# Moving one set of weight sums forward on GpSimd, and one column copy's engine, in a chunked attention with a Fourier mix and an MLP

## The chip, the cores and the metric

The kernel runs on one core of a Trainium2 chip. The metric is the device time of one launch in microseconds (us); the median of three runs is compared. All arithmetic is in fp32.

## The reference

What is computed, cut to what matters:

```python
# attention inside chunks of 64 tokens; q, k, v are (8, 8, 576, 64)
scores = (q_c @ k_c^T) / sqrt(64)
attn = softmax(scores)                    # over the chunk's 64 keys
x = (attn @ v_c) -> (8, 576, 512)         # heads side by side
# Fourier mix
mixed = real(fft(fft(x, axis=1), axis=2))
u = x + mixed
# normalisation over 512, then an MLP 512 -> 2048 -> 512, and the sum
un = (u - mean(u)) / sqrt(var(u) + 1e-6)
out = u + relu(un @ w_ch1) @ w_ch2
```

The two weights arrive as float64 and are converted to fp32 on the chip.

## The kernel before

**Tiles and groups.** Tokens are handled in tiles of 128 rows. A batch has four tiles, two of kind "lo" and two of kind "hi"; every even batch is preceded by one tile of kind "rest", which holds the middle chunks of two batches. The list `tiles` has them in order, and `first[b]` is the index of the first tile of batch b: `first[1]` is 5, `first[2]` is 9, and tile 9 is ("rest", 2, 0). Group g of the MLP is the four tiles of batch g (the last group: the four rest tiles).

**Stages.** While TensorE works at the MLP of group g, the attention and the Fourier mix of the next batch are woven in between its steps. The counter `t` numbers the steps of all groups; `begin[g]` is the first step of group g, and `begin[1]` is 32. The order of instructions on each engine is the order in which the Python code issues them, since the schedule is written out by hand; every engine works through its own queue in that order. SP issues most of the transfers, ScalarE a few.

**Attention.** `att_T` turns q and k of the next tile: from tile 10 on VectorE transposes them (L416), and for a "lo" tile a column copy on GpSimd follows (L418). For tile 9 and below TensorE transposes them (L397) and ScalarE copies the result, with the column copy on ScalarE or GpSimd (L428 to L431). `att_S` makes the scores (`sc`, L448), `softmax` and `exponential` follow, `att_P` turns the result, `att_V` makes the output (`xp`, L498), which VectorE scales and writes to `xall` (L511 to L515). `load` fetches q and k of the tile after (L250 in its second form), each into a buffer that has only one copy, so that a load of q waits for the transpose of the q before it.

**The MLP with saved products.** Group 0 goes through the plain product (`up_first`, `down_plain`). The down product of group 0 fills four PSUM banks `dn`, and at its end VectorE adds the residual and evicts them (L1249); `store` then writes the tiles out, "lo" tiles with L1037, "hi" tiles with L1046, on SP's queue and in part on ScalarE's.

From group 1 on, both products use a scheme with seven half-size products in place of eight. It needs sums of blocks of both weights, which GpSimd makes once:

- `keep2(i)`, i = 0 to 3: four sums over blocks of the second weight (L1087), written to `xall` (odd i) or `yall` (even i) and from there stored to a table in DRAM by SP (L1091). It is a generator that yields after each sum.
- `keep1(pair)`, pair = 0 to 3: four sums over blocks of the first weight (L1069), two written over parts of the second weight's space in `wb` that is free by then, one in place in `wa`, one more in `wb`. Group 1 uses them from there, and `keep1_store` saves them for later groups (L1074).
- `combined`: the like sums of the activations, on VectorE (L1024 to L1026, and L1022 for the late part of group 1).

`up_halves(1)` begins with product 1, whose weight is the second sum of `keep1(0)`: its first products are `pb` (L1289), then `pa`. The banks `pa` and `pb` come from the same ring of four as the `dn` banks.

**Where the sums are issued.** Once all pieces of the weights are converted, each step advances `conv2` by three: this chain runs `keep2` in the order 1, 0, 3, 2. What is left of it is issued at the end of step `begin[1] - 1`, and after it `keep1(0)`; the other three sets of `keep1` follow at steps 33, 35 and 37:

```python
conv2 = iter([step for i in range(HF // 2) for step in [keep2(i ^ 1)]])
...
if t == begin[1] - 1:
    for _ in conv2:
        pass
if begin[1] - 1 <= t < begin[1] + 7 and t % 2:
    keep1((t - begin[1] + 1) // 2)
```

So GpSimd's queue has, in this order: `keep2(1)`, `keep2(0)`, `keep2(3)`, `keep2(2)` with a column copy (L418) in `keep2(3)`, a memset (L528) in `keep2(2)` and another column copy (L418) behind it, then `keep1(0)`, `keep1(1)`, `keep1(2)`, the row shifts of `shift` (L555), and `keep1(3)`.

Of the kernel before, what the change touches and what calls it, by code (L numbers as in the profile page):

```python
# [16 lines left out]
def kernel(  # L17
# [85 lines left out]
    NO, HF = 7, KF // 2  # L103
# [63 lines left out]
    tiles, first = [], []  # L167
# [27 lines left out]
    def kind(n):  # L195
        return tiles[n][0]
# [196 lines left out]
    def turn(src):  # L393

        pt = ps_t.tile([128, 4, 128], FP32, tag="pt", name="pt")
        for j in range(4):
            nc.tensor.transpose(pt[:, j, :], src(j), ident)  # L397
        return pt


    def att_T(n, which="qk"):

        if n > first[2]:
            for src, dst, nm in ((qs, qT, "qT"), (ks, kT, "kT")):
                if nm[0] not in which:
                    continue
                a = src.pop(n).rearrange("p j (t b d) -> p j t b d", t=4, b=2)[:, :, :, 0]  # L410
                t = one_p.tile([128, NJ, 2, CH + 1], FP32, tag=nm, name=nm)
                low = kind(n) == LO and nm == "qT"
                to = t[:, :, :, CH:0:-1] if low else t[:, :, :, 0:CH]
                if kind(n) == HI:
                    to = to[:, :, ::-1]
                nc.vector.transpose(out=to.rearrange("p j c (r t) -> p j t c r", t=4), in_=a)  # L416
                if low:
                    nc.gpsimd.tensor_copy(t[:, :, :, 0:1], t[:, :, :, CH:CH + 1])  # L418
                dst[n] = t.rearrange("p j c t -> p (j c) t")
            if n + 1 < NT:  # L420
                load(n + 1, which)
            return
        a = qs.pop(n)
        pt = turn(lambda j: a[:, 2 * j:2 * j + 2, :].rearrange("p h d -> p (h d)"))
        t = one_p.tile([128, 2 * NJ, CH + 1], FP32, tag="qT", name="qT")
        low = kind(n) == LO
        nc.scalar.copy(t[:, :, CH:0:-1] if low else t[:, :, 0:CH], pt.rearrange("p j (c t) -> p (j c) t", c=2))
        if low and n < first[1]:  # L428
            nc.scalar.copy(t[:, :, 0:1], t[:, :, CH:CH + 1])
        elif low:  # L430
            nc.gpsimd.tensor_copy(t[:, :, 0:1], t[:, :, CH:CH + 1])  # L431
        qT[n] = t
        a2 = ks.pop(n)
        pt = turn(lambda j: a2[:, 2 * j:2 * j + 2, :].rearrange("p h d -> p (h d)"))
        t = one_p.tile([128, NJ, 128], FP32, tag="kT", name="kT")
        nc.scalar.copy(t, pt)
        kT[n] = t.rearrange("p j (c t) -> p (j c) t", c=2)
        if first[1] <= n + 1 < NT:
            load(n + 1)
# [617 lines left out]
    def parts1(pair):  # L1057
        a11, a12, a21, a22 = w1_part(pair, 0, 0), w1_part(pair, 0, 2), w1_part(pair, 1, 0), w1_part(pair, 1, 2)
        o1, o2, o4 = (made1(pair, j) for j in range(3))
        return a11, o2, o1, a21, a12, o4, a22  # L1060

    def keep1(pair):

        a11, o2, o1, a21, a12, o4, a22 = parts1(pair)
        for out_, in0, in1, op in (
            (o1, a21, a22, ALU.add), (o2, o1, a11, ALU.subtract),
            (a21, a11, a21, ALU.subtract), (o4, a12, o2, ALU.subtract),
        ):
            nc.gpsimd.tensor_tensor(out=out_, in0=in0, in1=in1, op=op)  # L1069
# [6 lines left out]
    def keep2(i):  # L1076

        m = 2 * i
        b11, b12 = w2[:, m:m + 2, 0:HM], w2[:, m:m + 2, HM:DM]
        b21, b22 = w2[:, HF + m:HF + m + 2, 0:HM], w2[:, HF + m:HF + m + 2, HM:DM]  # L1080
        to = xall[:, 2 * G:2 * G + 4, 0:DM] if i % 2 else yall
        o1, o2, o3, o4 = (to[:, j].rearrange("p (m e) -> p m e", m=2) for j in range(4))
        for out_, in0, in1, op in (
            (o1, b12, b11, ALU.subtract), (o2, b22, o1, ALU.subtract),
            (o3, b22, b12, ALU.subtract), (o4, b21, o2, ALU.subtract),
        ):
            nc.gpsimd.tensor_tensor(out=out_, in0=in0, in1=in1, op=op)  # L1087
            yield
        to = s2.rearrange("o p (m e) -> o p m e", m=HF)
        for o, a in ((1, o2), (2, o1), (3, o3), (6, o4)):  # L1090
            nc.sync.dma_start(out=to[o, :, m:m + 2], in_=a)  # L1091
        yield

    def keep2_whole(i):

        m = 2 * i
        to = s2.rearrange("o p (m e) -> o p m e", m=HF)
        for o, m0, e0 in ((0, m, 0), (4, HF + m, 0), (5, HF + m, HM)):
            nc.sync.dma_start(out=to[o, :, m:m + 2], in_=w2[:, m0:m0 + 2, e0:e0 + HM])
# [331 lines left out]
    def mlp(g):  # L1431

        for h1 in up_halves(g) if g >= first_of[1] else up_plain(g) if g > 0 else up_first():
            yield
        yield from (down_few if g >= FEW else down_halves if g >= first_of[2] else down_plain)(g, h1)

    with tc.manual_schedule():
# [33 lines left out]
        def round_next(later=None):  # L1471
            nonlocal n_w
            if n_w <= len(pieces):
                round_weight(n_w, later)
                n_w += 1
# [22 lines left out]
        begin = [0]  # L1498
        for g in range(NG):
            begin.append(begin[-1] + (KF if g < first_of[1] else 2 * HF) + (KF if g < first_of[2] else 2 * NO if g < FEW else NR2 // 2))  # L1500
        ready_at = [begin[g] + (2 * KF - 7 if g < first_of[2] else 2 * HF + 4) for g in range(NG)]
        conv2 = iter([step for i in range(HF // 2) for step in [keep2(i ^ 1)]])

        def chain(gens):
            for gen in gens:
                yield from gen

        n_whole, n_kept, late, rest_ = 0, 0, [], None
        conv2 = chain(conv2)
        t = 0  # L1510
        for g in range(NG):
            for _ in mlp(g):
                t += 1
                heavy = False
                for do in late:
                    do()
                late = []
                if t == 8:
                    nc.scalar.copy(tk, early_tk[:, :, :, 0:NE])
                if cur < len(sides):  # L1520
                    t0 = 3 if cur == 0 else ready_at[cur - 1]
                    t1 = ready_at[cur]
                    due = min(sizes[cur], (t - t0) * sizes[cur] // (t1 - t0))
                    while done < due:
                        heavy = next(sides[cur], None) or heavy
                        done += 1
                    if t >= t1:
                        for _ in sides[cur]:
                            pass
                        cur, done = cur + 1, 0  # L1530
                if not heavy:
                    round_next(late if t < KF and t % 4 == 3 else None)
                    if t <= 2 or t < KF and t % 4 == 0 or t >= KF + 3:
                        round_next()

                while n_whole < HF // 2 and n_w > KF + HF + 2 * n_whole + 2:
                    keep2_whole(n_whole)
                    n_whole += 1
                if n_w > len(pieces):
                    for _ in range(3):  # L1540
                        next(conv2, None)
                if t == begin[1] - 1:
                    for _ in conv2:
                        pass
                if begin[1] - 1 <= t < begin[1] + 7 and t % 2:
                    keep1((t - begin[1] + 1) // 2)
                if t == ready_at[NG - 3]:
                    rest_ = make_rest()
                    next(rest_)
                if t > ready_at[NG - 3] + 4 and (t < begin[NG - 2] or t % 4 != 3):  # L1550
                    next(rest_, None)
                if t == begin[FEW] + 2:
                    more = [xall[:, 2 * G:2 * G + 4, :].rearrange("p a f -> p (a f)")[:, i * Z3:(i + 1) * Z3] for i in range(2)]
                    more += [one_p.tile([128, Z3], FP32, tag=tag, name="more") for tag in ("q", "k", "zf")]
                    slab3.extend(a.rearrange("p (m e) -> p m e", m=4) for a in more)
                if begin[FEW] + 2 <= t < begin[FEW] + 2 + NS3:
                    fetch(3)
                if begin[1] < t < begin[1] + KF:
                    for i in range(2):
                        if n_kept < HF // 2 * NO:  # L1560
                            keep1_store(n_kept)
                            n_kept += 1
                if t in (begin[1] + 9, begin[1] + 13, begin[1] + 16):
                    fetch(2)
                if t == begin[1] + KF:
                    for _ in range(NS1):
                        fetch(1)
# [49 lines left out]
```

## Time and profile before

| | |
|---|---|
| median of three runs | 1073.49 us (1072.22 to 1073.67) |
| the profiled execution, its own time | 1074.23 us |
| its span | 1072.2 us |
| TensorE busy | 1046.3 us, 98% of the span |
| VectorE busy | 610.8 us, 57% |
| GpSimd busy | 406.6 us, 38% |
| ScalarE busy | 315.3 us, 29% |
| end of group 0's down product on TensorE | 190.37 us |
| first product of group 1 on TensorE | 192.78 us |

The span reaches from the first instruction to the last; some 2 us of the time lie around it. The profile is one execution, so single rows are right for that execution, and the median of the runs may lie a little to either side. PE is TensorE, DVE VectorE, ACT ScalarE, POOL GpSimd; SPq and ACTq are the engines' issue queues. A time "at 190.37" is counted from the span's start. A share of busy time is an average over stages with different limits: what a change in one stage is worth is read from the waits of that stage.

### The profile page before, as it was taken

The numbers are of one execution on the slowest core, as the hardware profiler recorded it, in microseconds if no ns is written. First come the engines' busy times: TensorE is split into PE (matmuls) and PEld (weight loads), VectorE is DVE, ScalarE is ACT, GpSimd is POOL, SyncE is SP. The second block draws the span as 40 slices with busy tenths as digits, with TensorE's granted clock in tenths as the row PEclk, the third lists the DMA queues.
The fourth block names the chain that finished last, engine by engine and source line by source line (L and its number), as shares of the span: only waits on it lengthen the run. The fifth ranks groups of instructions, "written<-read, shape, count | busy, mean of one in ns | idle before, by whom it ended". The sixth has DMA issues, their size and how long they took to land.

```text
span 1072.2 us, 20212 instructions
## 1 busy us (share of the span) xinstructions
PE 1046.3 (98%) x7498; PEld 854.6 (80%) x7498; DVE 610.8 (57%) x1319; ACT 315.3 (29%) x746; POOL 406.6 (38%) x531
## 2 busy tenths in 40 slices
PE   8999989899999999999999999999999999999997
PEld 6645444688888888888888888788888888888886
DVE  4798986684567465664565554745664535433331
ACT  4688563233113411322032312331133103101200
POOL 4310018672415140344134321614161726780281
PEclk9999999999999999999999999999999999999999
DMA  8767565489668546883667266954654559776763
GB/s 176 232 186 218 123 196 189 139 249 312 233 199 232 149 140 198 239 232 119 191 209 231 99 182 195 231 165 163 202 177 116 208 191 350 229 231 199 272 228 106
DMA packets 157759, 212.74 MB, mean 198 GB/s; under 512 B 69308, under 2 KB 103100, under 8 KB 151390
## 3 DMA queue, kind: packets, MB, share of 16 engines
q1 hardware_dynamic: 154012, 208.04, 63.4%
q10 hardware_dynamic: 3330, 2.76, 1.1%
q8 instruction: 60, 0.98, 0.4%
q0 software_dynamic: 320, 0.66, 0.3%
q14 instruction: 37, 0.30, 0.1%
HBM read 177.31 MB, written 34.08 MB: 197 GB/s over the span
## 4 chain that ended last, share of the span: by engine, by line
PE 77%; DVE 8%; DMA 5%; ACT 4%; SPq 3%; issue 2%; POOL 1%; DVEq 0%; ACTq 0%; POOLq 0%
PE pa L1289 19%; PE pb L1341 18%; PE pb L1289 14%; PE pa L1341 13%; PE dn L1405 4%; PE pt L397 2%; PE mix L838 2%; DMA xall<-in_moe_w_ch_dram 1%; SPq L263 1%; PE xp L498 1%; PE z L719 1%; DVE power L378 1%; DMA out_dram<-o 1%; PE sc L448 1%; DMA v<-in_v_dram 1%
## 5 line engine op out<-in xcount | busy, mean ns | idle before, releaser
L1289 PE MATMUL pa<-unT,wa 128*128 128x256 f32 x736 | 175.0, 381 | 2.5 <-DVE wa L1297 2.5
L1289 PEld LDWEIGHTS pa<-unT,wa 128*128 128x128 f32 x736 | 138.3, 190 | 21.8 <-DVE wa L1297 2.7
L1289 PE MATMUL pb<-wa 128*128 128x256 f32 x448 | 106.9, 381 | 0.1
L1341 PE MATMUL pa<-wb,h 128*128 128x256 f32 x448 | 101.5, 380 | 0.0
L1341 PE MATMUL pb<-wb,h 128*128 128x256 f32 x448 | 100.7, 379 | 0.0
L1289 PEld LDWEIGHTS pb<-wa 128*128 128x128 f32 x448 | 84.1, 190 | 12.3 <-DVE h L1299 0.5
L1341 PEld LDWEIGHTS pa<-wb,h 128*128 128x128 f32 x448 | 83.9, 190 | 11.3
L1341 PEld LDWEIGHTS pb<-wb,h 128*128 128x128 f32 x448 | 84.1, 190 | 11.0
L1169 POOL TENSOR_TENSOR h<-h 128x256 f32<-128x256 f32 x56 | 47.7, 860 | 102.3 <-DVE wb L1167 98.2
L555 POOL COPY xall<-xall 1x512 f32<-1x512 f32 x28 | 17.8, 636 | 154.3 <-DVE xall L515 126.9
L1295 DVE TENSOR_TENSOR wa<-pb,wa 128x256 f32<-128x256 f32 x56 | 23.8, 425 | 69.7 <-ACT wa L1294 69.7
L1289 PE MATMUL pb<-unT,wa 128*128 128x256 f32 x256 | 60.5, 379 | 0.0
L1303 ACT ACTIVATE h<-pa 128x256 f32<-128x256 f32 x64 | 24.6, 384 | 114.1 <-PE pa L1289 113.6
L1236 PE MATMUL dn<-wb,h 128*128 128x512 f32 x128 | 57.5, 597 | 0.0
L1294 ACT COPY wa<-pa 128x256 f32<-128x256 f32 x56 | 20.9, 372 | 123.5 <-PE pa L1289 80.6
L1289 PEld LDWEIGHTS pb<-unT,wa 128*128 128x128 f32 x256 | 48.6, 190 | 6.6
L1289 PE MATMUL pa<-wa 128*128 128x256 f32 x224 | 53.9, 383 | 0.0
L1309 ACT ACTIVATE h<-h 128x512 f32<-128x512 f32 x64 | 39.6, 629 | 45.0 <-DVE h L1308 44.8
L1341 PE MATMUL pb<-wb,yall 128*128 128x256 f32 x224 | 51.2, 381 | 0.0
L1341 PE MATMUL pa<-wb,yall 128*128 128x256 f32 x224 | 50.6, 379 | 0.3 <-DMA wb<-s 0.3
L1341 PE MATMUL pb<-wb 128*128 128x256 f32 x224 | 50.7, 379 | 0.0
L1195 PE MATMUL up<-unT,wa 128*128 128x512 f32 x108 | 49.4, 598 | 0.0
(299 smaller groups left out, 1976.1 us busy)
## 6 DMA issues: line engine op xcount, KB each, us to landing
wb<-s SPq DMA_DIRECT2D x49, 1024.0 KB
wa<-s SPq DMA_DIRECT2D x196, 256.0 KB
xall<-in_moe_w_ch_dram SPq DMA_DIRECT2D x22, 512.0 KB
q<-in_q_dram SPq DMA_DIRECT2D x96, 112.0 KB
k<-in_k_dram SPq DMA_DIRECT2D x96, 112.0 KB
wb<-s SPq DMA_DIRECT2D x16, 512.0 KB
v<-in_v_dram SPq DMA_DIRECT2D x124, 64.0 KB
s<-part SPq DMA_DIRECT2D x30, 256.0 KB
```

What stands on the lines that cost most here:

```text
L397: nc.tensor.transpose(pt[:, j, :], src(j), ident)
L838: nc.tensor.matmul(out=mix[:, cols], lhsT=zt[:, T], rhs=tab, start=(T == 0), stop=(T == 3), skip_group_check=True,)
L1169: nc.gpsimd.tensor_tensor(out=h1[:, m, hi], in0=h1[:, m, lo], in1=h1[:, m, hi], op=ALU.subtract)
L1195: nc.tensor.matmul(out=up, lhsT=w1[:, kk, m * 128:(m + 1) * 128], rhs=unT[:, kk], start=(kk == 0), stop=(kk == KD - 1), skip_group_check=True,
L1236: nc.tensor.matmul(out=dn, lhsT=h1[:, m, s * 128:(s + 1) * 128], rhs=w2[:, m, :], start=(m == 0), stop=(m == KF - 1),)
L1289: nc.tensor.matmul(out=dst, lhsT=w[:, kk, r], rhs=rhs[o][:, kk], start=(o in (0, 1) and kk == 0), stop=(kk == 1), skip_group_check=True,)
L1294: nc.scalar.copy(a, dst)
L1295: nc.vector.tensor_tensor(out=b, in0=pbs[r][:, 0], in1=a, op=ALU.add)
L1303: nc.scalar.activation(out=h1[:, m, lo], in_=dst, func=ACTF.Relu)
L1309: nc.scalar.activation(out=h1[:, HF + m], in_=h1[:, HF + m], func=ACTF.Relu)
L1341: nc.tensor.matmul(out=dst, lhsT=lhs[:, m], rhs=w[:, m], start=(o in (0, 2) and m == 0), stop=(m == HF - 1), skip_group_check=True,)
L1405: nc.tensor.matmul(out=dst, lhsT=lhs[:, m], rhs=w[:, m], start=(fresh and not half and m == 0), stop=(m == 3), skip_group_check=True,)
```

## The change

`keep1(0)` becomes part of the chain `conv2`, between the second and the third set of `keep2`, as one step. The condition at the end of the step starts after `begin[1]`, so that it issues the sets 1 to 3 alone. The condition that picks ScalarE for the column copy in `att_T` gets a second alternative, `n == first[2]`.

```diff
-        if low and n < first[1]:
+        if low and (n < first[1] or n == first[2]):
             nc.scalar.copy(t[:, :, 0:1], t[:, :, CH:CH + 1])
         elif low:
             nc.gpsimd.tensor_copy(t[:, :, 0:1], t[:, :, CH:CH + 1])
...
-        conv2 = iter([step for i in range(HF // 2) for step in [keep2(i ^ 1)]])
+        def first_sums():
+            keep1(0)
+            yield
+
+        conv2 = iter([keep2(1), keep2(0), first_sums(), keep2(3), keep2(2)])
...
-                if begin[1] - 1 <= t < begin[1] + 7 and t % 2:
+                if begin[1] < t < begin[1] + 7 and t % 2:
                     keep1((t - begin[1] + 1) // 2)
```

As built, GpSimd's queue then has `keep2(1)`, `keep2(0)`, `keep1(0)`, `keep2(3)` with the column copy behind its first sum, `keep2(2)`, the second column copy, and `keep1(1)` on as before. On SP the four loads of k for tile 11 (L250) move ahead of the four stores of `keep2(3)` (L1091). The lists of TensorE, VectorE and ScalarE keep their order.

## The prediction

> **What bounds the kernel now.** I read the page first:
>
> ```profile
> PE 1046.3 (98%) x7498; PEld 854.6 (80%) x7498; DVE 610.8 (57%) x1319; ACT 315.3 (29%) x746; POOL 406.6 (38%) x531
> ```
>
> TensorE (PE) is busy for 98% of the span, so only its gaps can move the time. The waits of PE, from 190 us to the end, name them (columns: who waited for whom, total us, times, longest):
>
> ```profile
> PE pa L1289 <- DVE wa L1297: 2.5, 1, 2.5
> PE pb L1289 <- POOL wb L1069: 2.4, 1, 2.4
> PE sc L448 <- DVE kT L416: 0.7, 1, 0.7
> ```
>
> The second is the target: at 190.37 us PE is through with group 0's down product and waits until 192.78 for the first sums of `keep1(0)`. The timeline of GpSimd (POOL) there (start, us, engine, line, ...; idle time before, and its releaser, in brackets):
>
> ```profile
> 180.77 1.26 POOL L1087 TENSOR_TENSOR yall<-wb 128x512 f32<-128x512 f32 x1
> 182.11 1.33 POOL L1087 TENSOR_TENSOR yall<-wb,yall 128x512 f32<-128x512 f32 x1
> 183.40 1.44 POOL L1087 TENSOR_TENSOR yall<-wb 128x512 f32<-128x512 f32 x1
> ...
> 189.97 0.20 POOL L418 COPY qT<-qT 128x8 f32<-128x8 f32 x1 [3.72 <-DVE qT L416]
> 190.12 1.27 POOL L1069 TENSOR_TENSOR wb<-wa 128x512 f32<-128x512 f32 x1
> 191.47 1.26 POOL L1069 TENSOR_TENSOR wb<-wb,wa 128x512 f32<-128x512 f32 x1
> ```
>
> The reader is to see the 3.72 us of idle time: POOL has done its last `keep2` by 186.25, and `keep1(0)` stands behind a column copy (L418) that waits for VectorE (DVE). DVE's timeline over the same stretch:
>
> ```profile
> 181.70 0.61 DVE L1024 TENSOR_TENSOR xall<-unT 128x256 f32<-128x256 f32 x1 [8.07 <-ACT unT L1007]
> 182.35 1.37 DVE L1025 TENSOR_TENSOR xall<-unT,xall 128x256 f32<-128x256 f32 x1
> 183.64 1.48 DVE L1026 TENSOR_TENSOR unT<-unT 128x256 f32<-128x256 f32 x1
> ...
> 187.59 0.42 DVE L1024 TENSOR_TENSOR xall<-unT 128x256 f32<-128x256 f32 x1
> 188.05 0.42 DVE L1025 TENSOR_TENSOR xall<-unT,xall 128x256 f32<-128x256 f32 x1
> 188.39 0.42 DVE L1026 TENSOR_TENSOR unT<-unT 128x256 f32<-128x256 f32 x1
> 188.73 1.11 DVE L416 STREAM_TRANSPOSE qT<-q 128x512 f32<-128x512 f32 x1
> 189.67 2.47 DVE L1249 TENSOR_TENSOR o<-dn,xall 128x512 f32<-128x512 f32 x4
> ```
>
> The same three instructions (L1024 to L1026) take 0.61, 1.37 and 1.48 us while POOL works, and 0.42 each in POOL's idle time. L1025 ends at 183.72 and L1026 at 185.12, each 0.28 after the end of the POOL sum beside it (183.44 and 184.84). Last, from the chain of waits:
>
> ```profile
> 195.48 7.65 DMA out_dram<-o
> ...
> 204.01 7.00 DMA k<-in_k_dram
> ...
> 211.13 0.06 DVE kT L416
> ```
>
> PE's next gap (score product `sc` at 212.28) hangs on a load of k that lands at 211.01, behind the stores of group 0's output, and these follow the L1249 evictions.
>
> **What the Trainium skill says.** "SBUF — State Buffer", section "Who interferes with whom": a DVE instruction with two SBUF inputs contends with a GpSimd instruction that reads SBUF, and the one that comes second waits for the whole of the first. The trace agrees, with the 0.42 against 1.37 and 1.48 us above; L1249 and L1295 have one input in PSUM, and keep their 0.68 and 0.42 us beside POOL. "DMA: Bandwidth & Descriptors", section "Why a DMA increments its semaphore by 16 and not by 1": a copy runs on as many engines (up to 16) as divide its slowest dimension. L1037 stores 2x32x512, so two. The trace agrees that it is slow: four stores of 128 KB issued from 194.81 on land at 200.6, 203.1, 206.0 and 209.4 (landing records of the trace), and the k loads behind them take 7 to 8 us where those issued at 217.7 take 2.5 to 3.
>
> **The change, part by part.**
>
> *The column copy.* `first[2]` is tile 9, ("rest", 2, 0); the branch asks for kind "lo". The condition is never true. The built order agrees: ScalarE (ACT) has the same 600 rows, POOL still both L418 copies. Cost 0, with no cover needed.
>
> *The order on POOL.* The four sums of `keep1(0)` go ahead of `keep2(3)` and `keep2(2)`; no instruction is added or removed. Before, POOL ends `keep2(0)` at 175.6. The weights' last conversion and the stores that read those blocks are over by 162 and 165 us (DVE's timeline; landing records), and the products that read them longer still, so I charge the new waits nothing. Beside an idle DVE four such sums take 5.03 us (the second set, 195.51 to 200.54): `keep1(0)` is done at 180.65. PE's reason to wait at 190.37 is gone: **-2.41 us**, if nothing else comes late.
>
> *The first L418 copy* moves from 178.15 to about 181.85, ends at 182.05, and `sc` at 182.13 now waits for it, with the last two steps of the down product queued behind it on PE. A gain is excluded, as the copy only gets later; 0 to +0.3 us, I take 0.
>
> *What comes late instead.* Eight `keep2` sums start at 180.63 instead of 175.60. By the durations above: `keep2(3)` 180.63 to 186.2 with L418 inside, `keep2(2)` sums from 186.15, 187.5, 188.75 and 190.15, the last ending at about 191.6. So POOL is busy where it was idle. DVE's first L1024 to L1026 ends at 185.1 as before, each locked to a POOL sum then too; its next work reads PSUM and ends at 187.6. The second L1024 starts at 187.6, some 0.1 after a POOL sum: held to 188.75 + 0.28 = 189.0. L1025 is held by the next to 190.5, L1026 by the last to 191.9. Before, it ended at 188.81: **+3.1 us** on DVE. If L1024 slips in ahead of a sum, one hold less: +1.6. I take 3.1, as the start is set by DVE and POOL from one point (the end of the POOL sum beside L1026), 2.75 us on for DVE and 2.65 for POOL.
>
> *Behind it on DVE* stand L416 (1.11 us) and L1249 x4. The first L1249 ended at 190.35; now at 193.4. PE's first product of group 1 takes over that PSUM bank, so PE starts at 193.45 and not at 192.78: **+0.7 us**. The 2.41 is not won.
>
> *The queues.* On SP the first `keep2(3)` stores move behind the k loads of tile 11, the v loads and the `yall` stores follow 3 to 4 us later, to about 192.0; then come the q loads of tile 12 (189.86 before), which wait for L416 anyway, until 192.9. The tables that the late stores fill are read after 239 us, so their lateness costs nothing; were they not done by then, the slab's wait (0.3 us at 261) would grow. Output stores on ACT's and SP's queues wait for L1249: all 3.1 later, the four slow L1037 included. The k loads queue behind them and land at 211.0 + 3.1 = 214.1; L416 takes 1.1; `sc` starts at 215.4 instead of 212.28. PE arrives there at about 212.2, so its gap grows from 0.7 to 3.1: together **+3.1 us at 212**. From here PE, DVE and SP keep their spacing, and I find no slack: later PE gaps in the list are 2.5, 0.6, 0.3 and 0.3, each tied to work that shifts too. Less 0.1 for the last small one, +3.0.
>
> Other engines: POOL's second and later `keep1` sets start at about 193 instead of 195.5, and wait at L555 for DVE as before (6.5 us idle there): nothing won. ACT: its DMA issues end at 196.5 and not 193.4, just as the copy after PE's first `pa` falls due; covered by the same 3 us.
>
> **Sum.** The profiled execution took 1074.23 us (span 1072.2 and 2.0 around it), 0.74 above the median 1073.49 of the three runs. +3.0 gives 1077.2 for it, and **1076.5** against the median. 0.2%, or 2.1 us, is about what a measurement of this kernel can tell from no change.
>
> **Rivals.**
> 1. *The wait is won and kept: faster.* If DVE's instructions passed between POOL's sums as fast as in its idle time, PE would go on at 190.45, 2.3 us early. For it to last, the k load would have to land 2.3 us earlier too, though the evictions that release the stores end no earlier. It decides if k lands by about 208.7. 1073.5 - 2.3 = 1071.2. For it: only the 2.4 in the list. 6 in 100.
> 2. *Won and given back: no difference.* No hold on DVE, k still lands at 211: the gap at `sc` grows from 0.7 to 3.0. 1073.5. 10 in 100.
> 3. *One hold less.* DVE +1.6, k at 212.6: 1075.1. 14 in 100.
> 4. *More than the shift.* The late `yall` stores share the engines with the slow output stores, or another load meets them: up to +4.5, 1078. 10 in 100.
> 5. *The forecast:* +2.0 to +3.6, 60 in 100. That the copy does nothing is part of each case.
>
> **How the numbers follow.** Slower by over 0.2%: nearly all of the forecast (57), case 4 (10), a little of case 3 (2): 0.69. Within: the rest of both (3 and 12) and case 2: 0.25. Faster: 0.06. The range reaches from case 2 to the top of case 4: 1073.4 to 1078.4; it leaves out case 1, about half of case 2 with the scatter of the runs (1.45 us), and a little above. The likeliest case alone: 1075.5 to 1077.1.
>
> **What would show it.** Right: no wait of `pb` L1289 on POOL; the second L1024 to L1026 at over 1 us each, the first L1249 at about 192.7; the k loads landing near 214; a wait of `sc` on kT of about 3 us. Wrong: the second L1026 done by 189 (rival 1 or 2), or k landing near 211 in spite of late evictions (then the stores don't set it), or a new gap of PE after 216.

## The result and the profile after

| | median | runs |
|---|---|---|
| before | 1074.39 us (1071.4 to 1078.24) | 20 |
| after | 1076.63 us (1073.48 to 1079.26) | 20 |

The ratio is 1.0018, with a 95% interval of 1.001 to 1.0026: slower by 1.9 us (1.1 to 2.8; the two medians of the table differ by 2.2). That is just under the 0.2% that the prediction named as the limit of a measurement, so its likeliest outcome, slower by more than 0.2%, is neither shown nor excluded. The forecast of 1076.5 us had been made against a median of 1073.49 of three runs; as a step it was +3.0, and the measured step is two thirds of it. That 1076.5 lies so near the median of 1076.63 is luck: over 20 runs the median of before is 0.9 us higher than over three. The profiled execution of the changed kernel took 1077.03 us with a span of 1075.0, that is 2.8 over the span of before.

PE's waits of the changed kernel, from 190 us to the end (who waited for whom, total us, times, longest):

```profile
PE sc L448 <- DVE kT L416: 3.4, 1, 3.4
PE pb L1289 <- DVE o L1249: 3.0, 1, 3.0
PE pa L1289 <- DVE wa L1297: 1.8, 1, 1.8
```

`pb` no longer waits for POOL. It waits longer than before, 3.0 us and not 2.4, for the eviction L1249 on VectorE, and the wait of `sc` for its kT has grown from 0.7 to 3.4. The three small waits that closed the list of before are gone:

```profile
PE pb L1289 <- DVE h L1308: 0.6, 1, 0.6
PE pb L1289 <- DVE h L1299: 0.3, 1, 0.3
PE pa L1341 <- DMA wb<-s: 0.3, 1, 0.3
```

GpSimd's timeline of the changed kernel at that place (start, us, engine, line, operation; idle time before, and its releaser, in brackets):

```profile
187.30 1.26 POOL L1087 TENSOR_TENSOR yall<-wb,yall 128x512 f32<-128x512 f32 x1
188.51 0.09 POOL L528 MEMSET xall<- 128x1 f32 x1
188.57 1.40 POOL L1087 TENSOR_TENSOR yall<-wb 128x512 f32<-128x512 f32 x1
189.93 1.44 POOL L1087 TENSOR_TENSOR yall<-wb,yall 128x512 f32<-128x512 f32 x1
192.80 0.20 POOL L418 COPY qT<-qT 128x8 f32<-128x8 f32 x1 [1.43 <-DVE qT L416]
```

VectorE's, over the same stretch:

```profile
187.43 1.42 DVE L1024 TENSOR_TENSOR xall<-unT 128x256 f32<-128x256 f32 x1
188.88 1.37 DVE L1025 TENSOR_TENSOR xall<-unT,xall 128x256 f32<-128x256 f32 x1
190.18 1.48 DVE L1026 TENSOR_TENSOR unT<-unT 128x256 f32<-128x256 f32 x1
191.58 1.09 DVE L416 STREAM_TRANSPOSE qT<-q 128x512 f32<-128x512 f32 x1
```

Read the two together. Each of the three VectorE instructions ends 0.28 or 0.29 us after the end of a POOL sum (188.85 after 188.56, 190.25 after 189.97, 191.66 after 191.37), and where they took 0.42 us each in POOL's idle time, they now take 1.37 to 1.48. VectorE comes 2.85 us later to L416 and to the evictions behind it. The chain of waits of the changed kernel shows what that carries along:

```profile
198.32 8.35 DMA out_dram<-o
...
206.68 0.34 SPq L250
...
207.54 6.66 DMA k<-in_k_dram
...
214.32 1.09 DVE kT L416
...
215.46 0.71 PE sc L448 x32
216.18 3.54 PE pa L1289 x8
```

The output store of L1037 is issued at 198.32 and lands at 206.67, SyncE issues the second of the four k loads (L250) 0.01 us later, the last of them lands at 214.20, and `sc` starts at 215.46. The last of these lines holds what the prediction did not have: eight `pa` products take 3.54 us where eight take 1.73 elsewhere. A table by windows of the changed kernel says why (us of the window, busy time and number of instructions by engine, granted TensorE clock, DMA share, GB/s):

```profile
212.00:216.00 4.00, 0.57 (x36) 0.54 (x32) 1.68 (x5) 0.00 (x0) 0.00 (x0) 1.00 0.45 136
216.00:219.40 3.40, 3.40 (x20) 2.68 (x12) 2.70 (x8) 0.63 (x1) 1.91 (x4) 0.50 0.89 259
219.40:226.00 6.60, 6.60 (x31) 5.53 (x30) 5.73 (x8) 0.77 (x2) 6.52 (x6) 1.00 0.89 269
```

After the gap at `sc`, TensorE ran at half its clock for 3.4 us (granted clock 0.50 in the middle row). In before, the clock at the like place, 213.00 to 216.40, was 1.00.

### The profile page after: what moved, and what is told of

Its sections match the earlier page's. It is cut to its first block, busy times and chain, and to the rows that moved or that the text cites. A ratio compares the mean times of both kernels' runs of the same rounds, so it can differ in the third digit from the quotient of the medians.

```text
span 1075.0 us, 20209 instructions
## 1 busy us (share of the span) xinstructions
PE 1048.0 (97%) x7498; PEld 856.6 (80%) x7498; DVE 612.2 (57%) x1319; ACT 315.3 (29%) x746; POOL 407.9 (38%) x531
## 4 chain that ended last, share of the span: by engine, by line
PE 81%; DMA 5%; DVE 5%; ACT 4%; SPq 2%; POOL 1%; issue 1%; DVEq 0%; ACTq 0%; POOLq 0%
PE pa L1289 20%; PE pb L1341 18%; PE pb L1289 15%; PE pa L1341 14%; PE dn L1405 4%; PE pt L397 2%; PE mix L838 2%; PE z L719 1%; PE xp L498 1%; DMA v<-in_v_dram 1%; DMA xall<-in_moe_w_ch_dram 1%; PE sc L448 1%; PE up L1195 1%; SPq L263 1%; DMA out_dram<-o 1%
## 5 line engine op out<-in xcount | busy, mean ns | idle before, releaser
L1341 PE MATMUL pa<-wb,h 128*128 128x256 f32 x448 | 101.5, 380 | 0.0
L1341 PE MATMUL pb<-wb,h 128*128 128x256 f32 x448 | 100.7, 379 | 0.0
L1341 PEld LDWEIGHTS pa<-wb,h 128*128 128x128 f32 x448 | 83.9, 190 | 11.3
L1341 PEld LDWEIGHTS pb<-wb,h 128*128 128x128 f32 x448 | 84.1, 190 | 11.0
L1341 PE MATMUL pb<-wb,yall 128*128 128x256 f32 x224 | 51.2, 381 | 0.0
L1341 PE MATMUL pb<-wb 128*128 128x256 f32 x224 | 50.7, 379 | 0.0
L1341 PE MATMUL pa<-wb,yall 128*128 128x256 f32 x224 | 50.5, 379 | 0.0
```

What stands on the lines that cost most here:

```text
L1341: nc.tensor.matmul(out=dst, lhsT=lhs[:, m], rhs=w[:, m], start=(o in (0, 2) and m == 0), stop=(m == HF - 1), skip_group_check=True,)
```

## The experiments

In every experiment the kernel before ran beside it on the same chip, in five rounds; the ratio is against those runs. "At 212" below is the start of the `sc` product that begins at 212.28 us in the profile of before. The times of landings are the landing records of the traces.

**1. Is it VectorE's hold, or something else in the new order?** The changed kernel, with the order, the waits and the stores of `keep2` kept, but without the eight sums of `keep2(3)` and `keep2(2)`. It leaves out that part of the computation.

```diff
-            nc.gpsimd.tensor_tensor(out=out_, in0=in0, in1=in1, op=op)
+            if i < 2:
+                nc.gpsimd.tensor_tensor(out=out_, in0=in0, in1=in1, op=op)
```

> The changed kernel without the eight GpSimd sums of keep2(3) and keep2(2); their stores stay, so SP issues the same (the tables of half the second weight then hold other data). Theory (held VectorE): GpSimd is idle from 181 to 189, the second L1024 to L1026 take 0.42 us each, the first L1249 starts near 189.7, pb starts at 190.4 and not 193.2, k lands near 211 again, sc waits about 3.0 us for kT: 0 +-0.8 us against before, 2 us less than the changed kernel. Rival (the order on SP or the added waits are what costs, not the sums beside VectorE): L1249 stays near 192.5 and the time at +2. Rival (the wait removed is a gain that lasts): -2.3.

Measured: 1073.72 us against 1073.94, ratio 1.0000 (0.9991 to 1.0009). The loss is gone, and with it the hold: L1024 to L1026 take 0.43, 0.43 and 0.42 us again, and `pb` starts at 190.96, 1.8 us ahead of before. But nothing is won. PE's first wait of this kernel after 190 us:

```profile
PE sc L448 <- DVE kT L416: 2.5, 1, 2.5
```

`sc` starts at 212.28, to 0.01 us where it did in before. So the sums are what makes the changed kernel slower, and here the gain at `pb` alone is taken back in full at `sc`, since k still lands at 211.0.

**2 to 4. Does SyncE's order carry the wait at `sc`?** Group 0's twelve output stores, issued behind VectorE's evictions so far, were collected in a list and issued at the end of step `begin[1] + 1`, behind the loads of that step: once in the changed kernel, once in the kernel before, and once in the changed kernel with `keep2(3)` and `keep2(2)` issued behind the second column copy as well.

```diff
-                    store(n, o)
+                    put_by.append((n, o))
...
+                if t == begin[1] + 1:
+                    for n_o in put_by:
+                        store(*n_o)
```

> The changed kernel with the twelve output stores of group 0 issued one step later, behind the loads of k for tile 12. Theory: VectorE is held as before (L1249 at 192.5, pb at 193.2), but k no longer queues behind the slow stores: it lands by 205, sc waits nothing; the small VectorE waits of before (0.3 and 0.6) may go too. Against before: +0.5 at pb, -0.7 at sc, so -0.2 to -1.5 us. Rival (k is late for another reason, such as its own wait for the transpose of the k before, or the loads being slow by themselves): k lands near 214, the wait stays over 2.5 us, +2.

> The kernel before with the same twelve stores issued behind the loads of k for tile 12. Theory: pb still waits 2.4 us for keep1(0), k lands by 204, the 0.7 us at sc and the 3.7 us idle of VectorE before kT go: -0.7 to -1.6 us. Rival (stores don't set k): 0.

> The changed kernel with keep2(3) and keep2(2) issued behind the second column copy, so that GpSimd is idle beside L1024 to L1026, and with the output stores behind the k loads. Theory: pb starts at 190.4, nothing waits at sc: -2.4 -0.7 and up to -0.8 for the small waits, so -2.5 to -4 us against before. Rival (something else comes late, such as keep1(1) at 203 or the write of xall row 8 that waits for the late store of keep2(3)): a new wait of PE in 198 to 210, -1 or less.

Measured: 1078.37 (ratio 1.0039, 1.0028 to 1.0051), 1077.99 (1.0038, 1.0025 to 1.0052) and 1078.35 us (1.0043, 1.0029 to 1.0057), all against 1073.94. All three missed. In each of them k landed by 206 and `sc` had no wait, and each lost time elsewhere. In the first, a stretch at half clock came right behind the gap at `pb` (193.7 to 197.1), and `sc` started at 213.67, 1.4 us later than in before. In the second, `sc` stood 0.7 us ahead, as expected. In the third, `pb` stood 2.1 and `sc` 3.0 us ahead, and then came the largest wait of all, in PE's list of that kernel:

```profile
PE pb L1289 <- DVE h L1308: 6.7, 1, 6.7
```

VectorE's queue was held there by L416, which waited 7.5 us for a load of q. SyncE issued this load only at 219.74: the transfers ahead of it in its queue (L1074, L273) had waited 4.7 us in all for output stores to land, and the four slow L1037 stores landed from 209.7 to 217.7. In the first two, the next wait was at 261 us, at the first L1341: 2.3 us for ScalarE's L775 in the first, 2.2 us for the load of the saved sums (`wb<-s`) in the second. So in the third, the slow store that was moved out of the way of one load stood in the way of the next; for the waits at 261 the traces don't show a chain back to the stores.

**5. Are sums on POOL enough by themselves?** The kernel before, with three further sums of the same size on GpSimd ahead of the second column copy, into two rows of `xall` that nothing reads.

```diff
+                if t == 30:
+                    for j in (2, 3, 2):
+                        nc.gpsimd.tensor_tensor(
+                            out=xall[:, 2 * G + j, 0:DM], in0=w2[:, 12], in1=w2[:, 13], op=ALU.subtract,
+                        )
```

> The kernel before with three more GpSimd sums (two SBUF inputs, results unused) in the 3.7 us of GpSimd's idle time ahead of the second column copy; nothing else moves. Theory: the second L1024 to L1026 are held (the first two over 1 us each), the first L1249 starts at 191.5 or later instead of 189.7, k lands about 2 us later and the wait at sc stays with all of it behind: +1.5 to +3 us. Rival (VectorE isn't held; what cost was the order on SP or the later stores of keep2): L1249 at 189.7, 0.

Measured: 1076.56 us against 1073.88, ratio 1.0022 (1.0014 to 1.0031). VectorE's timeline of this kernel:

```profile
189.14 1.40 DVE L1024 TENSOR_TENSOR xall<-unT 128x256 f32<-128x256 f32 x1
190.57 1.37 DVE L1025 TENSOR_TENSOR xall<-unT,xall 128x256 f32<-128x256 f32 x1
191.87 0.41 DVE L1026 TENSOR_TENSOR unT<-unT 128x256 f32<-128x256 f32 x1
```

Two of the three are held. The third starts where POOL has just become free, and takes 0.41 us. Nothing is reordered here, so sums on POOL are enough to hold VectorE and to make the kernel slower. That the loss is as large as that of the change says less: it came another way. The second column copy waited on POOL for the held VectorE's L416 until 193.42, `keep1(0)` stood behind it, and `pb` waited 4.3 us for POOL (2.4 in before). A stretch of 6.8 us at half clock began in that gap, and `sc` had no wait.

**6. Is it POOL at work, or POOL reading?** The same place, with eight memsets of the same tiles in place of the three sums, so that GpSimd is busy without reading SBUF.

```diff
+                if t == 30:
+                    for j in (2, 3, 2, 3, 2, 3, 2, 3):
+                        nc.gpsimd.memset(xall[:, 2 * G + j, 0:DM], 0.0)
```

> The kernel before with eight GpSimd memsets of 128x512 in the same place: GpSimd is busy but reads no SBUF. Theory: L1024 to L1026 keep 0.42 us each, the first L1249 stays at 189.7, 0 (a little more if the memsets outlast the idle time). Rival (any work of GpSimd there holds VectorE, or what counts is that GpSimd comes late to keep1(0)): L1024 to L1026 over 0.6 us, +1 or more.

Measured: 1073.81 us against 1073.88, ratio 0.9997 (0.9987 to 1.0007). The timelines of POOL and of VectorE in this kernel:

```profile
185.99 3.78 POOL L1544 MEMSET xall<- 128x512 f32 x8
```

```profile
187.45 0.42 DVE L1024 TENSOR_TENSOR xall<-unT 128x256 f32<-128x256 f32 x1
187.91 0.42 DVE L1025 TENSOR_TENSOR xall<-unT,xall 128x256 f32<-128x256 f32 x1
188.25 0.42 DVE L1026 TENSOR_TENSOR unT<-unT 128x256 f32<-128x256 f32 x1
```

All three run inside the 3.78 us of memsets, at the same 0.42 us as in POOL's idle time. A GpSimd that is busy with memsets does not hold VectorE; one that reads SBUF does. That is the sentence of the Trainium skill that the prediction rested on ("SBUF — State Buffer", section "Who interferes with whom"), which speaks of a GpSimd instruction that reads, not of one that only writes; with experiments 1 and 5 both halves of it are shown here.

**7 and 8. The four slow stores alone, spread out.** Group 0's four L1037 stores were issued from ScalarE, one for each step from `begin[1] + 1` on: in the kernel before, and in the changed kernel with both late sets of `keep2` behind the second column copy.

```diff
-                nc.sync.dma_start(out=to, in_=o[r0:r0 + CH])
+                if n in groups[0]:
+                    put_by.append((to, o[r0:r0 + CH]))
+                else:
+                    nc.sync.dma_start(out=to, in_=o[r0:r0 + CH])
...
+                if t > begin[1] and put_by:
+                    to, from_ = put_by.pop(0)
+                    nc.scalar.dma_start(out=to, in_=from_)
```

> The kernel before with the four slow stores of group 0 (L1037) taken off SP's queue and issued from ScalarE, one per step from step 33 on; the other eight stay where they were. Theory: k lands by 205, sc waits nothing, VectorE's 3.7 us idle before kT goes; at 261 the slab's wait is what the earlier try to move the stores ran into, so it must stay under 1 us: -0.5 to -1.5. Rival (the slow stores block SP's later loads wherever they are, by holding engines): a new wait in 215 to 265, +1 to +4.

> The changed kernel with keep2(3) and keep2(2) behind the second column copy (GpSimd idle beside L1024 to L1026), and the four slow stores spread from ScalarE as in the run before. Theory: pb at 190.5, no wait at sc, so 3 us ahead at 212; -2 to -3.5 at the end if the slab at 261 comes as early. Rival: SP is the limit between 205 and 261, so that PE gives the 3 us back at the slab: 0 to -1.

Measured: 1076.11 us (ratio 1.0022, 1.0013 to 1.0031) and 1079.69 us (1.0055, 1.0037 to 1.0073), both against 1073.88. Both missed. The stores took 6 to 10 us to land, as before, but now among the k loads: k landed at 213.9 and at 218.2 instead of 211.0, and `sc` waited 2.1 and 7.3 us. The traces show that a k load also left SyncE late. In experiment 7 the first and the third left at 204.96 and 207.49, right behind the landing of a slow store (204.90 and 207.47) whose semaphore the load is to use next. The second k load of before (203.15, behind a landing at 203.14) and of the changed kernel had waited in the same way. In experiment 8 the stores of the late `keep2` sets, ahead of the k loads on SyncE, waited for slow stores and for POOL, and the first k load left only at 208.69, where it had left at 202.15 in before.

**9 and 10. The slow stores from GpSimd's queue.** One line in the kernel before, and the same in the changed kernel:

```diff
-                nc.sync.dma_start(out=to, in_=o[r0:r0 + CH])
+                (nc.gpsimd if n in groups[0] else nc.sync).dma_start(out=to, in_=o[r0:r0 + CH])
```

> The kernel before, with one edit: the four slow stores of L1037 for group 0's tiles are issued from GpSimd's queue and no longer from SyncE's and ScalarE's, where the k loads for the product sc stood behind them. Theory A (the k loads are late because they stand behind these stores in a queue, as both spread-out versions still left them): the k loads land by about 205 us and not at 211, sc at 212 has no wait (0.7 us less), pb still waits 2.4 us for keep1(0); the stores go out behind GpSimd's keep1(0), which costs GpSimd less than 1 us. Sum -0.7, and up to -1 more if no gap is followed by a stretch at half clock: 1072.5 to 1073.5 against 1073.9. Theory B (the slow stores hold up the loads on the engines that they share, whichever queue issues them): k lands at 210 or later, or another load is caught: 0 to +4 us.

> The changed kernel, with the same edit: group 0's four slow L1037 stores from GpSimd's queue. The hold on VectorE stays, so pb still waits 3.0 us for the eviction L1249 and stands +0.5 us against before. Theory A (the lateness at sc is carried by the stores ahead of the k loads): sc has no wait, so the +3.2 us at 212 becomes -0.2 (pb's +0.5 less sc's old 0.7), and the half clock of 216 to 219 us goes with the gap: -0.5 to -2 us against before at the end, about 1072.5; the changed kernel is then no longer slower. Theory B (shared engines): k still lands after 213 and the result stays at +1 to +3.

Measured: 1073.62 us (ratio 0.9998, 0.999 to 1.0007) and 1074.43 us (0.9999, 0.999 to 1.0007), both against 1074.16. In the kernel before, the first three k loads were issued 3.0 to 3.7 us earlier than they had been and still landed at 209.4 to 210.1, around the end of the last slow store (209.66), the fourth at 210.4: at 212 it is 0.6 us ahead, with no wait, and the end shows nothing of it. So it isn't the issuing queue, SyncE alone in before, that holds the k loads back (theory A falls there). What is under way when they arrive fits all the traces: in experiment 3, where the slow stores were issued after them, the four k loads took 2.2 to 2.8 us each, where they take 7.0 to 7.9 in before. In the changed kernel the stores were issued from 193.90 on (197.63 without the edit), the last landed at 207.15 and k at 209.62. `sc` did not wait any more:

```profile
PE pb L1289 <- DVE o L1249: 3.0, 1, 3.0
...
PE pa L1289 <- ACT xall L1294: 1.0, 1, 1.0
```

It started 1.2 us later than in before and not 0.2 earlier, since a new wait of 1.0 us came in at 197 (ScalarE stood at its fourth L1046 issue for 2.5 us); the hold and its wait at `pb` are still there. The changed kernel is no longer slower, though: the larger part of its loss ran through the k loads. With the gap at `sc`, the stretch at half clock behind it is gone too.

**11 and 12. POOL out of VectorE's way, with and without the store edit.** The changed kernel, with `keep2(2)` issued after the second column copy, just ahead of `keep1(1)`. Experiment 11 has the store edit of 9 and 10 too; 12 has this edit alone.

```diff
-        conv2 = iter([keep2(1), keep2(0), first_sums(), keep2(3), keep2(2)])
+        conv2 = iter([keep2(1), keep2(0), first_sums(), keep2(3)])
...
+                if t == begin[1] + 1:
+                    for _ in keep2(2):
+                        pass
```

> The changed kernel with two edits: keep2(2) is issued after the second column copy, just ahead of keep1(1), and not straight behind keep2(3); and group 0's four slow L1037 stores leave from GpSimd's queue. GpSimd is then idle beside VectorE's second L1024 to L1026. Theory A: these take 0.42 us each again, the first L1249 ends at about 190.4, pb goes on at 190.4 to 190.9 without the old 2.4 us wait, and sc has no wait either: 3 us ahead of before at 212. If nothing else catches it, -2 to -3.5 us: 1070.5 to 1072. Theory B (a gain before 212 is always given back): the late keep2(2) stores or keep1's later sets become the next wait, a gap at 216 to 262 us of 2 us and more appears, and the end is at 0 to +4 us.

> The changed kernel with one of the two edits of the last run: keep2(2) is issued after the second column copy, just ahead of keep1(1); the slow L1037 stores stay where they are. Theory A (both waits count, and sc's follows the output stores, which follow the evictions; the evictions are as early as before, no earlier): pb goes on at about 190.3, 2.5 us early, without a wait; the k loads land at 211 to 212 as before, so sc waits 3 us instead of 0.7 and starts at 212.3; a stretch at half clock may follow that gap (+1.6). Sum 0 to +1.5 against before; together with the run before it this shows that neither edit is worth anything alone. Theory B (the store edit contributed little, the order alone carries the gain): sc starts at 210 to 211 and the end is -2 to -4 us.

Measured: experiment 11 took **1069.57 us** (6 runs) against 1074.16 (27 runs), ratio 0.9960 (0.9949 to 0.9972), faster than both kernels; experiment 12 took 1073.23 against 1073.38, ratio 0.9998 (0.9987 to 1.0008). POOL's timeline of experiment 11, and then VectorE's:

```profile
185.92 0.09 POOL L528 MEMSET xall<- 128x1 f32 x1
189.77 0.20 POOL L418 COPY qT<-qT 128x8 f32<-128x8 f32 x1 [3.76 <-DVE qT L416]
190.46 2.72 POOL L1037 DMA_DIRECT2D out_dram<-o  x4 [0.48 <-DVE o L1249]
193.19 1.28 POOL L1087 TENSOR_TENSOR yall<-wb 128x512 f32<-128x512 f32 x1
```

```profile
187.41 0.42 DVE L1024 TENSOR_TENSOR xall<-unT 128x256 f32<-128x256 f32 x1
187.86 0.43 DVE L1025 TENSOR_TENSOR xall<-unT,xall 128x256 f32<-128x256 f32 x1
188.21 0.42 DVE L1026 TENSOR_TENSOR unT<-unT 128x256 f32<-128x256 f32 x1
```

POOL's 3.76 us of idle time are back, the three instructions pass in them, and the four stores leave POOL right behind the evictions. All of PE's waits after 190 us in this kernel:

```profile
PE pa L1289 <- DVE wa L1297: 2.0, 2, 1.8
PE pa L1289 <- ACT xall L1294: 0.8, 1, 0.8
PE pb L1289 <- DVE h L1308: 0.6, 1, 0.6
PE pb L1289 <- DVE h L1299: 0.2, 1, 0.2
```

No `pb` on POOL or on L1249, no `sc` on kT: `pb` starts at 190.22, `sc` at 209.92 (2.4 us ahead), and PE is 2.9 us ahead just after 261 and 3.8 at 964. The last 0.9 us fall far behind the places of the two edits, and no run shows why. In experiment 12 `pb` is early as well (190.10), and `sc` at 210.16, with a wait of 1.3 us and not the 3 that I expected, because SyncE's slow stores left 2 us earlier (192.69 and not 194.81); k landed at 208.9. In before, the third of the q loads ahead of these stores had been held on SyncE until a store of ScalarE's queue landed at 193.91, which uses the same semaphore (S104 in the trace). With `keep2(2)`'s four stores gone from this place the q loads have other semaphores, and the third left at 190.88. At 261 the load of the saved sums caught PE:

```profile
PE pa L1341 <- DMA wb<-s: 1.2, 1, 1.2
```

Of the 2.7 us at `pb`, 1.2 were left there in this profile, and nothing in the median over the runs. So against before neither edit showed a gain alone (ratios of 0.9998 to 0.9999 in experiments 9, 10 and 12), and together they bring 0.4%, 4.6 us in the medians. Two waits in series, at `pb` and at `sc`, both stood in the way.

## Why the prediction held, and which of its terms were off

**Held, with the numbers.** `keep1(0)` ended at 180.39 (180.65 expected) and the wait of `pb` on POOL went. The last `keep2(2)` sum ended at 191.37 (191.6), the second L1026 at 191.66 (191.9), `pb` started at 193.24 (193.45), k landed by 214.20 (214.1), `sc` started at 215.46 (215.4). The whole run stood 0.24 us earlier at 172 already, which is the common offset of the first ones. All of the three holds came, so the rival with one hold less falls, and those without a hold fall with experiment 1 against the result itself. Experiment 10 bears out the second half of the chain, from the evictions over the stores to the k loads. The new condition for the column copy did nothing that the trace shows: both L418 copies stand on POOL as before. It was not run on its own.

**Off: "From here PE, DVE and SP keep their spacing, and I find no slack".** Between `sc` and the end, four waits shrank or went:

| PE's wait | before | after |
|---|---|---|
| `pb` on L1299 and L1308, 219 to 223 us | 0.3 + 0.6 | none |
| first L1341 on the load `wb<-s`, 261 us | 0.3 | none |
| `pa` on L1297, 673 us | 2.5 | 1.8 |

That is 1.9 us given back, where the prediction allowed 0.1. This is the term of the sum that was wrong: I took it that each of these waits is "tied to work that shifts too". The work at 261 does not shift in full: with PE later, its load comes in time. The last row I would not build on, as that wait had 0.8 us in experiment 6 and 1.6 in 9, with nothing changed near it.

**Off: the clock.** "A new gap of PE after 216" was on my list of what would prove me wrong, but not that the old gap, once it was longer, would slow what follows it. The 3.4 us at half clock cost 1.6 us at 219 in this profile (eight `pa` products in 3.54 us, where the eight behind a `sc` take 1.92 later on); PE then came too late for the two small waits of the first row, which gave 0.9 of it back. That "only its gaps can move the time", as the prediction opens, leaves this out: PE's busy time grew here. The sum for the two profiled executions closes: 0.6 more wait at `pb`, 2.7 more at `sc`, 1.6 by the clock, less 1.9 given back and less the 0.24 of the start is 2.8, the difference of the spans. That the profiled time of 1077.03 us met the 1077.2 of the prediction's sum is two errors of opposite sign.

**The 2.8 us of the profiles and the 1.9 of the medians.** Both lie within the interval of 1.1 to 2.8, and single executions of either kernel are spread over 6 to 7 us, so the two figures don't contradict each other. The clock suggests itself as a reason: the profile of before had no half clock ahead of its last microsecond. Every run lists its mean granted clock, and one stretch of 3.41 us at half clock takes 0.0016 off it. The mean over the 20 runs of after is 0.9964; over the runs of before that ran beside the experiments it is 0.9970 to 0.9974. By these means after has about half a stretch more in each run, an estimate. But what a stretch costs can't be read off them. In those 127 runs of before the time hardly follows the clock: the 31 with a clock of 0.999 or more have a median of 1073.4 us, the 48 with 0.996 or less one of 1074.1, though they have on average two stretches more. And the profile of the changed kernel has another stretch at 158 to 161 us: behind it PE stood 1.3 us later than in before, and at 172 it was 0.24 earlier again, since a wait of 1.4 us had gone. How much of the 1.9 us is the clock's stays open.

## What to carry to other kernels

Before an instruction of GpSimd is moved into its idle time, look at what VectorE does there: here its two-input work from SBUF ran more than three times as long beside GpSimd's sums, so idle time on GpSimd may be what a critical VectorE needs. Closing a gap on the engine that bounds can be worth nothing until the next gap behind it is closed too; here either edit alone gave nothing, and both gave 0.4%. A slow store that is put off is not removed: name the load that it will then be in flight with. Here the versions that put the stores behind or among the loads lost time at a later place (experiments 2 to 4, 7 and 8). And a transfer that was moved or dropped here also changed which semaphore later transfers share, and so which landing they waited for (experiments 9 and 12).

## What the runs showed of the hardware

- **Half clock after short gaps.** A stretch of 3.41 us at half TensorE clock began from 0.1 us ahead of the end of a gap to 1.3 us behind it in several traces, with gaps of 2.1 (experiment 7), 2.2 (3), 2.3 and 3.1 (2), 2.4 (6 and 7), 2.5 (1) and 3.4 us (after); with gaps of 4.3 (5), 6.7 (4) and 7.3 us (8) it began inside the gap and lasted 6.83 us. It did not come behind the 2.4 us in the profiles of before, of 3 and of 9, the 2.5 at 673 us in before, the 2.6 at 207 us in 8, nor behind the 3.0 at `pb` in after and in 10. So the length of the gap alone doesn't separate the two groups. How the gap lies on a fixed grid does: within a trace the stretches begin whole multiples of 3.413 us apart (157.98 and 216.01 in after, 17 of them). With this grid laid over each trace, from 170 to 1060 us, all 11 windows of it at full clock in which TensorE was idle for 62% or more were followed by half clock, and none that was idle for 57% or less; none lies between. (Earlier, one at 148 us in experiment 10 was followed by it at 55%.) In after the gap at `sc` took 84% of its window, and the one at `pb` 56% and 33% of two. The Trainium skill ("TensorE: Matmul & The Clock Gate", section "What's actually happening") tells of a free-running activity window of about 3.4 us, with which the grid agrees; the same page (section "Why this matters for your kernels") advises against gaps above about 3 us, and the gaps here were in part shorter.
- **The hold has a fixed tail.** A held L1024 to L1026 ends 0.28 us after the POOL sum that holds it, in before, in after and in experiment 5; the next POOL sum, which starts while VectorE is still at it, takes 1.33 to 1.45 us and not 1.26.
- **The loads that follow slow stores.** With the slow stores on SyncE, the last k load landed 1.56 us after the last of them in before and in experiments 1, 5, 6 and 12 (2.06 in after), though it had been issued 4.6 to 5.4 us before that store landed. From GpSimd's queue each of these stores has 16 landing records, spread over 4 to 8.5 us, where it has three from SyncE; they took 8 to 12 us from issue to landing, against 6 to 10 in before. They also have semaphores of their own there (S112 to S115), so that no k load waits for a slow store's landing before it is issued. Which of these makes experiment 11 work, the earlier issue, the spread or the semaphores, was not separated.
